# Other SBUF starts for the operands of gate and up: six forms of x and half of the forms of W

## The chip, the cores and the metric

The kernel runs on one core of a Trainium2 chip. The metric is the device time of one execution in microseconds; for the kernel before it is 1454.19 us, the median of three runs between 1452.14 and 1454.41. Engines are named as the profile names them: PE is TensorE, PEld its weight loads, DVE is VectorE, ACT is ScalarE, POOL is GpSimd, SP is SyncE. SBUF is the on-chip memory of 128 partitions; an address in this text is a byte offset within a partition, the same in all of them.

## The reference

A transformer block's two halves over 2048 tokens of 576 channels: linear attention with 32 heads, and a gated feed-forward of width 4608 whose output passes through silu and scales the attention.

```python
xn = _layernorm(x, axis=-1)
s = _A_ref(xn, A_wqkv, A_wo)          # linear attention
g = _silu(_B_ref(xn, B_w_gate, B_w_up, B_w_down))
return x + s * g

def _B_ref(x, w_gate, w_up, w_down):
    g = jnp.einsum("bsd,df->bsf", x, w_gate)
    u = jnp.einsum("bsd,df->bsf", x, w_up)
    h = _gelu(g) * u
    return jnp.einsum("bsf,fd->bsd", h, w_down)
```

All is in float32. The change touches the operands of the two products with `w_gate` and `w_up`.

## The kernel before

Matmuls run in float32r with each operand cut into a high and a low part, so that one product of 288 channels by something is 7 matmuls: a list of seven pairs (`PASSES`: part of W, part of x) over five parts of each operand. The parts of an x form lie behind each other in one tile of 5 x 512 words (2048 bytes a part); a W form has 5 x 128 words (512 bytes a part, 2560 bytes a form).

The stages follow each other on TensorE: k and v for 16 tiles of 128 tokens (`x_mm`, tiles `kv`), q, the attention's output (`s_mm`), then gate and up, then down (`down_mm`, tiles `bd`). All is issued in the program's order: helpers `act`, `vec`, `mm`, `pool` and `dma` (lines 141 to 153) pin each instruction to its place in its engine's stream, and the matmuls of gate and up stand in `product` (line 909).

Gate and up use Strassen's scheme in Winograd's form: for each of 36 matrices (18 groups of 256 columns, for gate and for up) `matrix` runs seven products, each for the two halves s = 1 and s = 0 of the tokens, with 512 columns: 7 x 2 x 7 = 98 matmuls a matrix, 3528 in all. W is the stationary operand, x the moving one. A product takes one of seven forms of W and one of seven forms of x, in this order: A11 with B11 (tile `al`), S2 with T2 (`be`), S1 with T1 (`ga`), S3 with T3 (`de`), A12 with B21 (`al`), S4 with B22 (`ga`), A22 with T4 (`de`). The forms of x are the same for all 36 matrices and stay in SBUF, fourteen tiles: those of s = 1 are named `xo_1_...` and built there (`build`, or `normalize` for the plain ones); those of s = 0 are named `xr_...` and brought back from HBM by `back` (B11, T2, T1, T3 issued by GpSimd, B21, B22, T4 by SyncE). In the profile's names buffer numbers are left out: `xo_T` stands for any T form of s = 1, `xr_T` for any of s = 0.

The forms of W are made anew for each matrix by `mat_sums` (GpSimd) and `cut_w` (ScalarE, VectorE) into two tiles that are used over and over: `wa` holds A11, S1, S2, S3 at places 0 to 3; `wb` holds A12 at place 1, S4 at place 3, and A22 at place 2 or 0 in turn.

SBUF is laid out by hand. `big(i, ...)` places a tile at the numbered place `i` of the pool; what stood there before must be done with first. Places 7 to 10 (`ODD`) start at an odd multiple of 128 bytes, and a tile there that leaves room begins `GAP` = 32 words (128 bytes) later. So all operands of gate, up and down start at a multiple of 256 bytes. `X_SLOT` and `X_BACK` say which form of x stands in which place.

In the k and v stage the moving operand is the weight: tiles `wkv` hold parts of 416 words, 1664 bytes, one behind the other, so that parts 0, 2, 4 start at a multiple of 256 bytes and parts 1, 3, 5 start 128 bytes beyond one. Each of the 16 tiles of tokens has three widths of columns, c = 0, 1, 2 (416, 412 and 388 columns), with 14 matmuls each, seven for each half of the channels. The seven passes read parts 0, 1, 3, 4, 0, 1 and 2 (`KV_PASSES`), so three of seven are off; the sixth piece of weight (c = 2, second half) has no tile of its own and lies in part 5 of the five others, so its seven are all off. Stationary operands (x) all start at multiples of 256 bytes there.

Of the kernel before, what the change touches and what calls it, by code (L numbers as in the profile page):

```python
# [9 lines left out]
F32R = mybir.dt.float32r  # L10
# [6 lines left out]
P = 128  # L17
# [8 lines left out]
TBN = S // TB  # L26
# [9 lines left out]

ODD = (7, 8, 9, 10)
GAP = 32
WP = 320
ODD_W = 9 * HALF  # L40
HEAD_W = 4 * WP + HALF

# [55 lines left out]
def block_kernel(ctx, tc, x, xe, xt, wq_d, wkv_d, wo, wgu_d, wd_d, out):  # L98
    nc = tc.nc
    sb = ctx.enter_context(tc.tile_pool(name="sb", bufs=1))  # L100
# [10 lines left out]
    def fold(t, dims):  # L111
        names = "abc"[: len(dims)]
        return t.rearrange(
            f"p ({' '.join(names)}) -> p {' '.join(names)}", **dict(zip(names[1:], dims[1:]))
        )

    def big(i, shape, dt, name):
        n = 1
        for d in shape[1:]:
            n *= d  # L120
        if i in ODD and n <= ODD_W - GAP:
            t = sb.tile([P, GAP + n], dt, tag=f"b{i}", bufs=1, name=name)
            return fold(t[:, GAP:], shape[1:])
        return sb.tile(shape, dt, tag=f"b{i}", bufs=1, name=name)

    def mid(i, shape, dt, name):
# [22 lines left out]
    def pool(op, *args, **kw):  # L149
        pin(getattr(nc.gpsimd, op)(*args, **kw))  # L150

    def dma(out, in_, eng=None):
        tc.keep_in_program_order((eng or nc.sync).dma_start(out=out, in_=in_))
# [21 lines left out]
    xo, xf, xstat, store = [{}, {}], [{}, {}], {}, {}  # L175

    def load_x(n, k):

        if n % 2 == 0:
            shape = [P, 2, 2, 3 * P] if n < TT else [P, 2, D + 6 * P]  # L180
            xstat[n // 2] = big(14 + n // 2 % 2, shape, F32, f"x_{n}")
        t = xstat[n // 2][:, n % 2 : n % 2 + k]
        if n == 0:
            for j in range(2):
                dma(out=t[:, 0, j], in_=xe[0:P, j], eng=(nc.sync, nc.scalar)[j])
        elif n < TT:
            dma(out=t, in_=xe[n * P : (n + k) * P].rearrange("(t p) j d -> p t j d", p=P))
        else:
            dma(out=t[:, :, 0:D], in_=x[n * P : (n + k) * P].rearrange("(t p) d -> p t d", p=P))
            dma(out=t[:, :, D:], in_=xt[n : n + k].rearrange("t p m -> p t m"))  # L190
# [75 lines left out]
    def new_plain(s, nm):  # L266
        at_ = XM[s][nm]
        xf[s][nm] = (mid if at_ < 3 else big)(at_, [P, 3, TBN], F32, f"xf_{s}_{nm}")

    def normalize(n, s, b, c):  # L270

        if n in xts:
            ms = xts.pop(n)
            m, r = (ms[:, None, i * P : (i + 1) * P] for i in range(2))
        else:
            m, r = rows_of.pop(n)
        xs = xstat[n // 2][:, n % 2, D:].rearrange("p (k t) -> p k t", k=6)
        vec("tensor_sub", xs, xs, m.to_broadcast([P, 6, P]))
        for j, nm in enumerate(BS[b]):
            if nm not in xo[s]:  # L280
                xo[s][nm] = big(2 * b + j, [P, 5, TBN], F32R, f"xo_{s}_{nm}")
                new_plain(s, nm)
            vec(
                "tensor_mul", xf[s][nm][:, :, c], xs[:, 3 * j : 3 * j + 3],
                r.to_broadcast([P, 3, P]),
            )
        for nm in BS[b]:
            to_operand(xo[s][nm], xf[s][nm], c)
# [37 lines left out]
    def to_operand(o, src, c):  # L326
        act(o[:, 0:3, c], src[:, :, c], AF.Copy)
        vec("tensor_sub", o[:, 3:5, c], src[:, 0:2, c], o[:, 0:2, c].bitcast(F32))
        vec("tensor_sub", 
            o[KR : 2 * KR, 2, c], src[KR : 2 * KR, 2, c], o[KR : 2 * KR, 2, c].bitcast(F32)  # L330
        )
# [16 lines left out]
    full = slice(0, TBN)  # L348

    def build(s, nm, i):  # L350
        xo[s][nm] = o = big(i, [P, 5, TBN], F32R, f"xo_{s}_{nm}")
        to_operand(o, xf[s][nm], full)
        return o

# [178 lines left out]
    def run(todo, n=None):  # L533
        for _ in range(len(todo) if n is None else min(n, len(todo))):
            todo.pop(0)()
# [153 lines left out]
    def kv_wo(gi):  # L689

        if gi == 4:
            at["kvh"] = big(4, [P, 4, 2, WP], F32R, "kvh")[:, :, :, 0:HALF]
            at["kvl"] = big(5, [P, 4, 2, WP], F32R, "kvl")[:, :, :, 0:HALF]

            at["kv4"] = big(6, [P, 4, 2, WP], F32R, "kv4")[:, :, :, 0:HALF]
            pool("memset", at["kv4"][Q4:P, 1].bitcast(F32), 0.0)
# [151 lines left out]
    raw, sums, wt = {}, {}, {}  # L848
    X = [{}, xo[1]]
# [235 lines left out]
    def ring(name, make):  # L1085
        if name not in early:
            early[name] = make()
        return early[name]
# [23 lines left out]
    def strided(t):  # L1112
        return bass.AP(
            tensor=t.tensor, offset=t.offset, ap=[list(t.ap[0]), [WP, 5], [1, HALF]]
        )
# [22 lines left out]
    def word_tiles(p):  # L1138
        if p not in word:
            n = len(word)  # L1140
            b = n % 2
            t = ring(("end", b), lambda: big((11, 4)[b], [P, 2, 4, WP], F32R, f"w_end{b}"))
            end = [t[:, i, :, 0:HALF] for i in range(2)]
# [182 lines left out]
    def down_all():  # L1326
# [59 lines left out]
        name=nc.get_next_instruction_name(), engine=mybir.EngineType.Activation,  # L1386
# [23 lines left out]
    _, mv0, st0 = mom[0]  # L1410
# [96 lines left out]
    for n in range(3, 2 * TT):  # L1507
# [3 lines left out]
        if n >= TT:  # L1511
            j, c = divmod(n - TT, 2)
# [18 lines left out]
    def form(nm):  # L1531
        keep(0, nm, build(0, nm, 12))
# [78 lines left out]
    X_BACK = {"B11": 13, "T2": 7, "T1": 8, "T3": 12, "B21": 4, "B22": 5, "T4": 6}  # L1611

    def back(*names, eng=nc.gpsimd):
        for nm in names:
            X[0][nm] = big(X_BACK[nm], [P, 5, TBN], F32R, f"xr_{nm}")
            dma(X[0][nm].bitcast(F32), store[0, nm], eng)

    def first_matrix():
# [5 lines left out]
    q_load(0, 7)  # L1624
    aside = {
        (2, 0): [lambda: den(3), lambda: build(1, "T1", X_SLOT["T1"])],
        (2, 1): [lambda: scale(3, 0, 1), lambda: halve(3, 0, 1)],
        (2, 2): [lambda: scale(3, 2, 3, 4), lambda: halve(3, 2, 3, 4)],
        (2, 3): [lambda: build(1, "T3", X_SLOT["T3"]), lambda: load_mat(0), lambda: q_load(1, 8)],
        (3, 0): [lambda: den(0), lambda: build(1, "T2", X_SLOT["T2"])],  # L1630
        (3, 1): [lambda: scale(0, 0, 1), lambda: halve(0, 0, 1), lambda: back("B11")],
        (3, 2): [lambda: scale(0, 2, 3, 4), lambda: halve(0, 2, 3, 4)],
        (3, 3): [lambda: build(1, "T4", X_SLOT["T4"]), lambda: back("T2")],
        (0, 0): [lambda: den(1)],
        (0, 1): [lambda: scale(1, 0, 1), lambda: halve(1, 0, 1)],
        (0, 2): [lambda: scale(1, 2, 3, 4), lambda: halve(1, 2, 3, 4)],
        (0, 3): [lambda: back("T1"), lambda: mat_sums(0)],
        (1, 0): [lambda: pieces.extend(first_matrix()), lambda: run(pieces[0])],
        (1, 1): [lambda: run(pieces[3])],
    }  # L1640
    pieces = []
    for tb in (2, 3, 0, 1):
        for t in range(TT):
            s_mm(tb, t)
            run(aside.get((tb, t), []))
    wt["b"] = big(14, [P, 4, 5, P], F32R, "wb")
    back("T3")
    run(pieces[4] + pieces[5])
    load_mat(1)
# [70 lines left out]
```

## Time and profile before

| what | value |
|---|---|
| median of the three runs | 1454.19 us |
| the profiled execution's own time | 1452.58 us |
| its span, first to last instruction of the program | 1450.9 us |
| gate and up on TensorE | 276.4 to 1075.8 us |
| down on TensorE | 1076 to 1446 us |
| granted TensorE clock over the span | 1.0 |

A row of the profile's groups names the line, the engine, the operation, what it writes and reads (out<-in), the shape and the count; behind the bar stand the busy time of the group, the mean duration of one in ns, and the idle time of the engine just before. Matmuls overlap on TensorE, so a group's busy time is the union of their durations, and the mean duration of one is longer than the time from one start to the next. A row of the windows view gives a stretch in us, its length, and for each engine (PE, PEld, DVE, ACT, POOL) busy time and count, then the granted clock, the DMA engines' share and GB/s.

### The profile page before, as it was taken

Reading aid. Unit: us, or ns where it says so; the run is one execution under the profiler, and the core shown is the slowest. Engines: PE = TensorE matmul, PEld = TensorE weight load, DVE = VectorE, ACT = ScalarE, POOL = GpSimd, SP = SyncE. Lnnn points to the kernel's source line nnn. Section 1 sums busy time; section 2 is a strip of 40 time slices with the busy share of each in tenths; the row PEclk is TensorE's granted clock in tenths of the full one; section 3 lists DMA queues with packets and bytes.
Section 4 is the critical chain, followed back from the end, with each engine's and each line's share of the span. In section 5 each row is a group of like instructions: output and inputs, shape, how many; then the busy total and the mean of one; then the engine's idle time right before and its main releaser. Section 6 shows DMA issues by size and latency. Waiting matters only on the chain.

```text
span 1450.9 us, 22169 instructions
## 1 busy us (share of the span) xinstructions
PE 1444.4 (100%) x8272; PEld 1286.5 (89%) x8272; DVE 1148.7 (79%) x1609; ACT 565.2 (39%) x918; POOL 580.1 (40%) x520
## 2 busy tenths in 40 slices
PE   9999999999999999999999999999999999999998
PEld 8989989988888888888888888888889999999998
DVE  7688666476787887887777878778888978989898
ACT  6444365333222233322332232332235556555454
POOL 3342340225756567566475754667632000000000
PEclk9999999999999999999999999999999999999999
DMA  5554115521532315224242243323379888767886
GB/s 221 186 205 158 45 36 207 224 95 51 171 101 100 131 52 188 88 95 140 72 159 87 97 150 102 117 87 121 126 272 347 269 261 252 249 188 235 278 293 225
DMA packets 119253, 235.04 MB, mean 162 GB/s; under 512 B 11658, under 2 KB 45354, under 8 KB 117226
## 3 DMA queue, kind: packets, MB, share of 16 engines
q1 hardware_dynamic: 116346, 221.37, 45.4%
q0 software_dynamic: 2656, 12.06, 2.2%
q8 instruction: 65, 1.06, 0.3%
q14 instruction: 42, 0.34, 0.1%
q10 hardware_dynamic: 144, 0.20, 0.0%
HBM read 150.96 MB, written 82.58 MB: 161 GB/s over the span
## 4 chain that ended last, share of the span: by engine, by line
PE 97%; DVE 1%; ACT 1%; issue 0%; POOL 0%; DVEq 0%; ACTq 0%; POOLq 0%
PE bd L147 25%; PE al L909 16%; PE ga L909 16%; PE de L909 16%; PE kv L147 8%; PE be L909 8%; PE s L147 4%; PE q L147 3%; PE kv_a L147 1%; PE idle L147 0%; PE d L147 0%; PE kw L147 0%; PE b L147 0%; ACT e_q L141 0%; PE xt L264 0%
## 5 line engine op out<-in xcount | busy, mean ns | idle before, releaser
L150 POOL TENSOR_TENSOR sm<-raw 128x384 f32<-128x384 f32 x72 | 75.0, 1041 | 144.0 <-DMA raw<-in_wgu_dram 125.8
L147 PE MATMUL kv<-wkv,xo_B 128*128 128x412 f32 (+2 forms) x662 | 125.0, 347 | 0.3 <-ACT xo_B L141 0.3
L147 PEld LDWEIGHTS kv<-wkv,xo_B 128*128 128x128 f32 x662 | 120.2, 188 | 1.7 <-ACT xo_B L141 0.9
L144 DVE TENSOR_TENSOR wa<-sm,wa 128x768 fp32r<-128x768 f32 x72 | 90.5, 1257 | 36.0 <-ACT wa L141 35.2
L147 PE MATMUL bd<-w_head,hi 128*128 128x288 f32 x516 | 117.5, 294 | 0.0
L144 DVE TENSOR_TENSOR wb<-raw,wb 128x256 fp32r<-128x256 f32 (+1 forms) x108 | 103.2, 955 | 7.2 <-ACT wb L141 5.5
L144 DVE TENSOR_TENSOR wa<-raw,wa 128x256 fp32r<-128x256 f32 x72 | 66.8, 928 | 50.6 <-ACT wa L141 47.4
L141 ACT ACTIVATE hi<-raw_h 128x1024 fp32r<-128x1024 f32 x59 | 62.5, 1059 | 96.1 <-PE bd L147 55.7
L147 PE MATMUL bd<-w_end,hi 128*128 128x288 f32 x448 | 89.4, 294 | 0.0
L141 ACT ACTIVATE spot_h<-spot_h 128x512 f32<-128x512 f32 x49 | 30.7, 633 | 150.1 <-DVE spot_h L144 150.1
L147 PEld LDWEIGHTS bd<-w_head,hi 128*128 128x128 f32 x516 | 86.8, 188 | 0.1
L144 DVE TENSOR_TENSOR raw_h<-raw_h,hi 128x1024 fp32r<-128x1024 f32 x59 | 71.8, 1221 | 18.8 <-ACT hi L141 18.8
L141 ACT ACTIVATE wa<-sm 128x1152 fp32r<-128x1152 f32 x36 | 41.8, 1161 | 92.8 <-PE de L909 92.8
L147 PE MATMUL bd<-w_end,raw_h 128*128 128x288 f32 x264 | 77.6, 294 | 0.0
L141 ACT ACTIVATE u<-al 128x512 f32<-128x512 f32 x72 | 41.0, 592 | 90.0 <-PE al L909 60.0
L147 PEld LDWEIGHTS bd<-w_end,hi 128*128 128x128 f32 x448 | 71.6, 188 | 0.0
L147 PE MATMUL bd<-beside,raw_h 128*128 128x288 f32 x240 | 70.5, 294 | 0.0
L150 POOL TENSOR_TENSOR spot_h<-spot_h,spot_h 128x512 f32<-128x512 f32 x45 | 62.8, 1403 | 2.9 <-DVE spot_h L144 2.4
L909 PE MATMUL al<-xo_B,wa 128*128 128x512 f32 x252 | 63.0, 389 | 0.0
L909 PE MATMUL al<-xr_B,wa 128*128 128x512 f32 x252 | 63.0, 389 | 0.0
L909 PE MATMUL be<-xo_T,wa 128*128 128x512 f32 x252 | 63.0, 389 | 0.0
L909 PE MATMUL be<-xr_T,wa 128*128 128x512 f32 x252 | 63.0, 389 | 0.0
(278 smaller groups left out, 4036.8 us busy)
## 6 DMA issues: line engine op xcount, KB each, us to landing
raw_h<-hs SPq DMA_DIRECT2D x176, 256.0 KB
raw<-in_wgu_dram SPq DMA_DIRECT2D x36, 768.0 KB
hs<-spot_h SPq DMA_DIRECT2D x90, 256.0 KB
hs<-spot_g SPq DMA_DIRECT2D x80, 256.0 KB
b<-in_wd_dram SPq DMA_DIRECT2D x42, 432.0 KB
hs<-spot_m SPq DMA_DIRECT2D x38, 256.0 KB
raw_g<-hs SPq DMA_DIRECT2D x22, 256.0 KB
raw_a<-hs SPq DMA_DIRECT2D x20, 256.0 KB
```

Of the source, the lines that this page charges most:

```text
L141: pin(nc.scalar.activation(*args, **kw))
L144: pin(getattr(nc.vector, op)(*args, **kw))
L147: pin(nc.tensor.matmul(*args, **kw))
L150: pin(getattr(nc.gpsimd, op)(*args, **kw))
L909: nc.tensor.matmul(o, w[0:rows, wi, :], xop[0:rows, xi, :], start=(start and n == 0), stop=(n == len(PASSES) - 1), skip_group_check=True,)
```

## The change

`big` takes a gap in words from its caller. A table `X_GAP` gives one for each place in which it matters; the forms of half s = 1 that `build` makes and those that `back` brings use it. Place 7 gets a gap of 0 where it had 32, places 8, 9 and 10 get 8, 16 and 24 words where they had 32, and places 12 and 13 get 8 and 16 where they had none. Tile `wb` is allocated with rows of 672 words for each form instead of 640, and the last 32 words of each are not used.

```diff
+X_GAP = {7: 0, 8: 8, 9: 16, 10: 24, 12: 8, 13: 16}
...
-    def big(i, shape, dt, name):
+    def big(i, shape, dt, name, gap=None):
...
-        if i in ODD and n <= ODD_W - GAP:
-            t = sb.tile([P, GAP + n], dt, tag=f"b{i}", bufs=1, name=name)
-            return fold(t[:, GAP:], shape[1:])
+        if gap is None and i in ODD and n <= ODD_W - GAP:
+            gap = GAP
+        if gap:
+            t = sb.tile([P, gap + n], dt, tag=f"b{i}", bufs=1, name=name)
+            return fold(t[:, gap:], shape[1:])
...
-        xo[s][nm] = o = big(i, [P, 5, TBN], F32R, f"xo_{s}_{nm}")
+        xo[s][nm] = o = big(i, [P, 5, TBN], F32R, f"xo_{s}_{nm}", X_GAP.get(i) if s else None)
...
-            X[0][nm] = big(X_BACK[nm], [P, 5, TBN], F32R, f"xr_{nm}")
+            i = X_BACK[nm]
+            X[0][nm] = big(i, [P, 5, TBN], F32R, f"xr_{nm}", X_GAP.get(i))
...
-    wt["b"] = big(14, [P, 4, 5, P], F32R, "wb")
+    wt["b"] = big(14, [P, 4, 5 * P + 32], F32R, "wb")[:, :, 0 : 5 * P].rearrange(
+        "p f (k c) -> p f k c", c=P
+    )
```

The places themselves stay where they were, and the order of the instructions on every engine, with their waits, stays the same. What moves are the starts, in bytes beyond a multiple of 256:

| operand | place | before | after |
|---|---|---|---|
| T1 of s = 1 (`xo_1_T1`) | 9 | 0 | 192 |
| T3 of s = 1 (`xo_1_T3`) | 10 | 0 | 224 |
| B11 of s = 0 (`xr_B11`) | 13 | 0 | 64 |
| T2 of s = 0 (`xr_T2`) | 7 | 0 | 128 |
| T1 of s = 0 (`xr_T1`) | 8 | 0 | 160 |
| T3 of s = 0 (`xr_T3`) | 12 | 0 | 32 |
| the other eight forms of x | | 0 | 0 |
| W in `wa`, and in `wb` at places 0 and 2 | 15, 14 | 0 | 0 |
| W in `wb` at places 1 and 3 (A12, S4) | 14 | 0 | 128 |

## The prediction

> **What bounds the kernel now.** The page comes first. Its head gives the span; its first part, TensorE's busy time; its clock row, whether the throttle cuts in; its fourth part, the chain of work that ended last.
>
> ```profile
> span 1450.9 us, 22169 instructions
> PE 1444.4 (100%) x8272; PEld 1286.5 (89%) x8272; DVE 1148.7 (79%) x1609; ACT 565.2 (39%) x918; POOL 580.1 (40%) x520
> ...
> PEclk9999999999999999999999999999999999999999
> ...
> PE 97%; DVE 1%; ACT 1%; issue 0%; POOL 0%; DVEq 0%; ACTq 0%; POOLq 0%
> ```
>
> TensorE is busy for 1444.4 of 1450.9 us at full granted clock, and 97% of the chain is matmuls. The view of waits, asked for TensorE alone, shows how little else there is. Its columns are total, times and longest.
>
> ```profile
> PE idle L147 <- POOL ident masks.py:199: 1.6, 1, 1.6
> PE kv L147 <- ACT xo_B L141: 0.3, 1, 0.3
> PE bd L147 <- DVE raw_h L144: 0.2, 1, 0.2
> ```
>
> TensorE waits 2.1 us in all, so the time is the sum of the intervals between matmuls. The windows view over the gate and up stage counts its matmuls and the busy time of each engine there (TensorE, weight loads, VectorE, ScalarE, GpSimd).
>
> ```profile
> 276.40:1075.80 799.40, 799.40 (x3528) 661.91 (x3527) 619.33 (x823) 235.13 (x384) 474.54 (x382) 1.00 0.35 119
> ```
>
> 799.40 us over 3528 matmuls is 226.6 ns each, 55% of the span. One nanosecond on each of them is 3.5 us. VectorE, the busiest helper, has 619.33 us of work there and so 180 us of slack.
>
> **What one matmul costs by its shape.** In the groups kept apart by shape the last figure before the idle time is the mean duration of one matmul. They are pipelined, so a duration is longer than an interval, but what lengthens the stream lengthens both.
>
> ```profile
> L909 PE MATMUL al<-xr_B,wa 128*128 128x512 f32 x252 | 63.0, 389 | 0.0
> ...
> L909 PE MATMUL ga<-xr_T,wa 128*128 128x512 f32 x252 | 63.0, 389 | 0.0
> ...
> L909 PE MATMUL al<-xo_B,wb 128*128 128x512 f32 x252 | 63.0, 389 | 0.0
> ...
> L147 PE MATMUL bd<-w_end,hi 128*128 128x288 f32 x448 | 89.4, 294 | 0.0
> ...
> L147 PE MATMUL kv<-wkv,xo_B 128*128 128x412 f32 x224 | 45.1, 352 | 0.0
> L147 PE MATMUL kv<-wkv,xo_B 128*128 128x416 f32 x214 | 43.2, 352 | 0.3 <-ACT xo_B L141 0.3
> L147 PE MATMUL kv<-wkv,xo_B 128*128 128x388 f32 x224 | 42.1, 338 | 0.0
> ```
>
> All operands of gate, up and down start at a multiple of 256 bytes today, and their durations have no spread: 389 ns whatever form or weight they read. (389 - 294) / (512 - 288) is 0.424 ns a column, which gives an aligned 388-column matmul 336.4 ns, a 412-column one 346.6 and a 416-column one 348.3.
>
> The k and v matmuls are what this trace has of the other kind. Their streamed operand lies in parts 1664 bytes apart, so every second part starts 128 bytes off a multiple of 256. Of the 14 matmuls of a tile with 412 or 416 columns 6 start off; of those with 388 columns 10 do, the last 7 in a row. They measure 338, 352 and 352 ns, which is 1.6, 5.4 and 3.7 ns above the line. The two wider shapes change between on and off inside every run, which gate and up will not do: there a form is streamed 7 times in a row. The nearest rows are therefore the last seven of a 388-column tile, all 128 off. Two such stretches, by tile, with the shortest, median and longest duration:
>
> ```profile
> L147 PE MATMUL kv<-wkv,xo_B x6: 333/336/336, 138.7 to 139.6; 128*128 128x388 f32 x6
> ```
>
> ```profile
> L147 PE MATMUL kv<-wkv,xo_B x4: 341/341/341, 131.5 to 132.1; 128*128 128x388 f32 x4
> ```
>
> The same weight parts in the same order, for two tiles of tokens: one runs at 336 ns, which is the aligned value, the other at 341 ns, 4.6 above it. Within a run the gait hardly changes.
>
> **The change part by part.** No engine's order of instructions changes; only addresses do. Their working, by class:
>
> *x off the grid.* With what each tile's base and gap add up to, T1 of half 1 starts 192 bytes beyond a multiple of 256 and its T3 224; of half 0, B11 starts at 64, T2 at 128, T1 at 160 and T3 at 32. Each is streamed 7 times in each of 36 matrices: 6 x 7 x 36 = 1512 matmuls. The price of one lies between no cost (the run at 336 ns) and 4.6 ns (341 ns), or 0 to 7.0 us in all. Below nothing: the shortest of the rows, 333 ns, is 3.4 under the line; a run that held it would save 1512 x 3.4 = 5.1 us. I take the mean of all 388-column matmuls, 1.6 ns, put on the 10 of 14 that start off: 2.2 ns, so 1512 x 2.2 = **3.3 us**.
>
> *W off the grid.* In the second weight tile the forms now lie 2688 bytes apart, so its places 1 and 3 (A12 and S4) start 128 off. They are stationary operands of 2 x 2 x 7 x 36 = 1008 other matmuls, whose x stays aligned. No matmul of the groups above loads a stationary operand from such a place. If only the distance between the two reads matters, they pay as above, 0 to 4.6 ns; if weight loads hide (661.91 us of them beside 799.40 us of matmuls), nothing; at the 3.4 ns below the line, -3.4 us. I take half of 2.2 ns: **1.1 us**.
>
> *Writers.* ScalarE and VectorE write the moved tiles in the same instructions. The W cuts would have to eat VectorE's 180 us of slack before TensorE waited: nothing. Without that cover a nanosecond there would be one here.
>
> *The four loads of kept forms.* GpSimd issues B11, T2, T1 and T3 of half 0, which get an odd start. By tile, the issue and landing of the three T, and TensorE's first use of two (T1 by ga, T3 by de); then GpSimd's timeline at T1's issue:
>
> ```profile
> L909 PE MATMUL ga<-xr_T,wa x7: 389/389/389, 284.3 to 285.7; 128*128 128x512 f32 x7
> ...
> L909 PE MATMUL de<-xr_T,wa x7: 389/389/389, 287.5 to 288.8; 128*128 128x512 f32 x7
> ...
> L153 POOL DMA_DIRECT2D xr_T<-kept_T x3: 527/536/567, 245.2 to 276.0; - x3
> ...
> DMA to landing us min/median/max: 6.4/6.9/7.8
> ```
>
> ```profile
> 261.97 0.53 POOL L153 DMA_DIRECT2D xr_T<-kept_T  x1 [16.26 <-PE s L147]
> ```
>
> The last, T3, is issued at 276.0 and lands by 283.8 at the latest, 3.7 us before its first matmul at 287.5. T1, issued at 262.0, has 14.5 us to spare, and the two before it are issued earlier still. A landing longer by a third would still be hidden by the matmuls before it: nothing; beyond that each us late is one of TensorE's.
>
> The sum is 3.3 + 1.1 = 4.4 us. The profiled execution took 1452.58 us (its span of 1450.9 and 1.7 around it), so it would become 1457.0; on the median of the runs, 1454.19, which lies 1.6 above it, **1458.6 us**.
>
> **Rivals.** *Addresses don't matter* (not slower). For it: the run at 336 ns pays nothing at 128 off; and the 388-column tiles, which have the largest share of odd starts, are nearest the line, so what the wider ones pay may come from changing parts, or from widths that are no multiple of 64. Against it: the 341 ns stretch, and that only the k and v rows have any spread. Time: 1454.2. The Trainium skill, "SBUF — State Buffer", Specifications (TRN2), has cache lines of 16 bytes as the unit at which a read pays, and under "Who interferes with whom" gives TensorE two read ports that never wait for anyone. All new starts are multiples of 32 bytes, so by that rule every operand crosses as many lines as before and the sum would be 0 instead of 4.4 us. The 336 ns run agrees with it; the 341 ns run doesn't.
>
> *Staggering pays* (faster). The aligned 512-column matmul has 389 - 512 x 0.424 = 172 ns of duration that is not streaming; a part of that may be weight load and stream meeting at the same place, each time alike, as all start on the same grid. If a distance between them took 3.4 ns off, as the 333 ns row shows once, the place would be the 1512 runs with moved x: -5.1 us, **1449.1**; with the 1008 of W, -8.6 us. It decides when weights of the next matmul no longer meet the stream. Against it: it is one of six, and the median of that run is the aligned value.
>
> *A whole further block is read.* If a read went in blocks of 256 bytes (64 columns), an aligned form is 8 blocks and a moved one 9: 64 x 0.424 = 27 ns, times 1512 = 41 us, **1495**. Against it: 388, 412 and 416 columns all touch 7 blocks, on or off the grid, yet 338 is far from 352.
>
> **How the numbers follow.** About 0.2%, 2.9 us, is what a measurement of this kernel can tell from no change. Forecast (moved reads pay 0 to 4.6 ns): 0.55; if all 2520 moved matmuls ran at the slow gait it would be 2520 x 4.6 = 11.6 us, so its own range is 1454.2 to 1465.8, and about 0.10 of it falls within 0.2%. No effect: 0.23. Staggering pays: 0.15, 0.02 of it too small to tell. A further block: 0.07. Slower is thus 0.45 + 0.07 = 0.52, the same 0.10 + 0.23 + 0.02 = 0.35, faster 0.13. The range runs from just above the second rival to the slow gait everywhere with the 2 us by which the runs of before spread: 1449.5 to 1468. It leaves out the further block and the ends of the others.
>
> **What would show it.** Right: in the groups by shape, the ten rows with a moved operand show other means than 389 ns (from wa: al of xr_B, be of xr_T, both ga and both de; from wb: both al and both ga), and the four others don't; the windows view of gate and up grows from 799.40 by some 4 us; the down stage keeps its time. A step is wrong if W's rows stay at 389 (the 1.1 us goes) or if unmoved forms slow down too, since then what counts is the change from run to run. If TensorE's waits grow beyond 2.1 us, a writer or a load is late and the costs that I set at nothing were not. Were all rows at 389, the first rival holds; below it, the second; near 416, the third.

## The result and the profile after

The changed kernel takes 1469.95 us (median of four runs, 1469.58 to 1470.39) where the kernel before takes 1453.74 (four runs, 1452.14 to 1454.41): 1.0113 times as long, with a 95% interval of 1.0096 to 1.0131. The forecast was slower, 1458.6 us, with a range that ended at 1468.0. The direction holds; the size is 16.2 us instead of 4.4.

The windows view of the kernel after, over gate and up and over down (TensorE, weight loads, VectorE, ScalarE, GpSimd, then clock, DMA share and GB/s):

```profile
276.60:1093.20 816.60, 816.60 (x3528) 662.28 (x3527) 622.00 (x824) 235.33 (x384) 473.64 (x382) 1.00 0.34 117
```

```profile
1093.60:1463.90 370.30, 369.72 (x2806) 369.25 (x2805) 330.84 (x384) 194.83 (x237) 19.53 (x26) 1.00 0.83 264
```

Gate and up took 799.40 us before and take 816.60 now, for the same 3528 matmuls at the same clock: 17.2 us, nearly all of the 17.8 by which the profiled span grew (1450.9 to 1468.7 us). Down keeps its time. TensorE's waits in the kernel after:

```profile
PE idle L150 <- POOL ident masks.py:199: 1.6, 1, 1.6
PE bd L150 <- DVE raw_h L147: 0.6, 2, 0.4
PE kv L150 <- ACT xo_B L144: 0.3, 1, 0.3
PE xt L267 <- PE idle L150: 0.3, 1, 0.3
```

They add up to 2.8 us and none lies in gate and up: nothing is late there. The matmuls themselves take longer, as the groups by shape show (busy time in us, then the mean duration of one in ns):

```profile
L912 PE MATMUL al<-xr_B,wb 128*128 128x512 f32 x252 | 64.7, 395 | 0.0
L912 PE MATMUL ga<-xr_T,wa 128*128 128x512 f32 x252 | 64.7, 396 | 0.0
L912 PE MATMUL de<-xo_T,wa 128*128 128x512 f32 x252 | 64.7, 396 | 0.0
...
L912 PE MATMUL be<-xr_T,wa 128*128 128x512 f32 x252 | 64.4, 394 | 0.0
...
L912 PE MATMUL al<-xr_B,wa 128*128 128x512 f32 x252 | 64.2, 394 | 0.0
L912 PE MATMUL be<-xo_T,wa 128*128 128x512 f32 x252 | 63.9, 392 | 0.0
L912 PE MATMUL de<-xo_T,wb 128*128 128x512 f32 x252 | 63.7, 392 | 0.0
L912 PE MATMUL al<-xo_B,wa 128*128 128x512 f32 x252 | 63.0, 389 | 0.0
L912 PE MATMUL de<-xr_T,wb 128*128 128x512 f32 x252 | 63.0, 389 | 0.0
```

All ten rows with a moved operand stand at 394 to 396 ns (five of them shown), whether x moved (by 32, 64, 128, 160, 192 or 224 bytes) or W (by 128). Their busy time is 1.2 to 1.7 us above 63.0, which over 252 matmuls is 4.8 to 6.7 ns each; all ten together lie 15.1 us above, 6.0 ns a matmul. Of the four unmoved rows two stay at 389 and two stand at 392: `be<-xo_T,wa` and `de<-xo_T,wb`, each of which follows a moved run. They add 1.6 us.

These are means. By tile, with the shortest, median and longest duration, one moved run (T2 of s = 0) and one unmoved run (T4 of s = 0):

```profile
L912 PE MATMUL be<-xr_T,wa x7: 387/395/398, 281.4 to 282.8; 128*128 128x512 f32 x7
...
L912 PE MATMUL de<-xr_T,wb x7: 389/389/389, 297.7 to 299.0; 128*128 128x512 f32 x7
```

The seven matmuls of a moved run do not pay alike, and a price per matmul, here and below, is a mean.

### The profile page after: what moved, and what is told of

It reads as the page before. It is cut to its first block, busy times and chain, and to the rows that moved or that the text cites. A ratio compares the mean times of both kernels' runs of the same rounds, so it can differ in the third digit from the quotient of the medians.

```text
span 1468.7 us, 22169 instructions
## 1 busy us (share of the span) xinstructions
PE 1461.6 (100%) x8272; PEld 1286.8 (88%) x8272; DVE 1150.7 (78%) x1609; ACT 565.7 (39%) x918; POOL 578.9 (39%) x520
## 4 chain that ended last, share of the span: by engine, by line
PE 96%; DVE 2%; ACT 1%; issue 0%; DMA 0%; POOL 0%; DVEq 0%; ACTq 0%; POOLq 0%
PE bd L150 23%; PE ga L912 16%; PE al L912 16%; PE de L912 16%; PE kv L150 8%; PE be L912 8%; PE s L150 4%; PE q L150 3%; PE kv_a L150 1%; PE idle L150 0%; PE d L150 0%; PE kw L150 0%; DMA raw_h<-hs 0%; DVE raw_h L147 0%; PE b L150 0%
## 5 line engine op out<-in xcount | busy, mean ns | idle before, releaser
L147 DVE TENSOR_TENSOR wa<-sm,wa 128x768 fp32r<-128x768 f32 x72 | 97.4, 1353 | 36.0 <-ACT wa L144 35.2
L147 DVE TENSOR_TENSOR wb<-raw,wb 128x256 fp32r<-128x256 f32 (+1 forms) x108 | 97.8, 906 | 7.4 <-ACT wb L144 5.8
L912 PE MATMUL al<-xr_B,wb 128*128 128x512 f32 x252 | 64.7, 395 | 0.0
L912 PE MATMUL ga<-xr_T,wa 128*128 128x512 f32 x252 | 64.7, 396 | 0.0
L912 PE MATMUL de<-xo_T,wa 128*128 128x512 f32 x252 | 64.7, 396 | 0.0
L912 PE MATMUL de<-xr_T,wa 128*128 128x512 f32 x252 | 64.6, 395 | 0.0
L912 PE MATMUL ga<-xr_B,wb 128*128 128x512 f32 x252 | 64.5, 395 | 0.0
```

The costliest lines, as they stand in the source:

```text
L147: pin(getattr(nc.vector, op)(*args, **kw))
L912: nc.tensor.matmul(o, w[0:rows, wi, :], xop[0:rows, xi, :], start=(start and n == 0), stop=(n == len(PASSES) - 1), skip_group_check=True,)
```

## The experiments

Three theories were put against each other. **Distance**: what counts is where the weights stand, within 256 bytes, against the stream beside which they are loaded. **Own start**: each operand that is off a multiple of 256 pays for itself. **Change**: what costs is that the place changes from run to run. All times below are medians; the kernel before ran on the same chip each time.

### x alone and W alone

The kernel after with one of its two parts undone:

```diff
 # x alone: the kernel after with
-    wt["b"] = big(14, [P, 4, 5 * P + 32], F32R, "wb")[:, :, 0 : 5 * P].rearrange(
-        "p f (k c) -> p f k c", c=P
-    )
+    wt["b"] = big(14, [P, 4, 5, P], F32R, "wb")
 # W alone: the kernel before with the reverse of this
```

> The six forms of x as in the change, the forms of W back at 2560 bytes. The changed kernel spends 17.2 us more on 2520 moved matmuls, 6.8 ns each. Theory 'distance' (a matmul pays when its moving operand and the stationary operand that is loaded beside it start at different places within 256 bytes): 1512 x 6.8 = 10.3 us more than before, 1464; the rows of the six moved runs at 394 to 396 ns, those from wb at 389 but for the one behind a moved run. Theory 'own start' (each operand off a multiple of 256 pays for itself): the same. Theory 'change' (what costs is that the place within 256 bytes changes from run to run): also some 10 us, but then runs of unmoved forms behind moved ones pay as much as moved ones.

> The forms of W 2688 bytes apart, all forms of x on multiples of 256. 'Distance' and 'own start': 1008 x 6.8 = 6.9 us more than before, 1460.6; the four rows of A12 and S4 at 394 to 395 ns, the others at 389 but for runs behind moved ones. My prediction had 1.1 us for this part. A sum of this and of the kernel with x alone near 17 us says that the two parts add up.

x alone takes 1464.49 us against 1453.26 (1.0076, 1.0059 to 1.0093), W alone 1459.02 (1.0040, 1.0025 to 1.0055): 11.2 and 5.8 us. They add up to 17.0, beside 16.2 for the whole change. With x alone the six moved rows stand at 394 to 396 ns and are 9.1 us of busy time above 63.0, 6.0 ns on each of 1512 matmuls; another 2.2 us lie in two unmoved rows right behind moved ones, `be<-xo_T,wa` (393 ns) and `al<-xo_B,wb` (394 ns). With W alone the four rows of A12 and S4 stand at 394 to 396 ns and all others at 389 to 391; 5.8 us is 5.7 ns on each of 1008.

W alone also shows which weights a stream meets. The places to look at are those where a run with weights on the grid (at multiples of 256 bytes) gives way to one with weights off, and back. First the timeline of W alone where S3 with `xr_T` (on) gives way to A12 (off), with start and duration in us; then the groups by shape in two windows of 0.07 us, at that place and where S4 (off) gives way to A22 (on):

```profile
512.71 0.62 PE L909 MATMUL de<-xr_T,wa 128*128 128x512 f32 x2
512.94 0.19 PEld L909 LDWEIGHTS al<-xo_B,wb 128*128 128x128 f32 x1
```

```profile
L909 PE MATMUL al<-xo_B,wb 128*128 128x512 f32 x1 | 0.4, 405 | 0.0
L909 PE MATMUL de<-xr_T,wa 128*128 128x512 f32 x1 | 0.4, 397 | 0.0
```

```profile
L909 PE MATMUL ga<-xr_B,wb 128*128 128x512 f32 x1 | 0.4, 390 | 0.0
L909 PE MATMUL de<-xo_T,wb 128*128 128x512 f32 x1 | 0.4, 389 | 0.0
```

The load for A12's first matmul begins at 512.94, while the last matmul of S3 streams. That matmul's own weights and x are on the grid, and it takes 397 ns. The last matmul of S4 works with weights that are off, while those loaded beside it are on the grid: 390 ns. Over the 36 matrices the last matmul of S3 takes 397 ns on average and the last of S4 takes 390. So a matmul pays for the weights of the **next** one.

### Everything shifted, and all of W shifted

```diff
 # everything 128 bytes later: the kernel before with
-    eps_t = sb.tile([P, 32], F32, name="eps_t")
+    eps_t = sb.tile([P, 64], F32, name="eps_t")
```

```diff
 # all forms of W 128 bytes later: the kernel before with
-        wt["a"] = big(15, [P, 4, 5, P], F32R, "wa")
+        t = big(15, [P, 32 + 4 * 640], F32R, "wa")[:, 32:]
+        wt["a"] = t.rearrange("p (f n) -> p f n", f=4)[:, :, 0 : 5 * P].rearrange(
+            "p f (k c) -> p f k c", c=P
+        )
 # and the same for wb
```

> The kernel before with its first small tile 128 bytes larger: every SBUF tile behind it moves by 128 bytes, so all operands of gate, up, down, q and s start 128 bytes beyond a multiple of 256, moving and stationary alike, and the distance between them stays. 'Distance': as before, 1453.7 within 2 us, gate and up at 389 ns. 'Own start': 3528 x 6.8 = 24 us more in gate and up alone, 1478 or later. 'Change': as before.

> The kernel before with both W tiles begun 128 bytes later: every stationary operand of gate and up starts 128 beyond a multiple of 256, every moving one on it, and nothing changes from run to run. 'Distance' and 'own start': 3528 x 6.8 = 24 us more, 1478; all fourteen rows at 394 to 396 ns. 'Change': as before, 1453.7, at 389 ns.

With everything shifted the time is 1453.41 against 1453.26 us: 1.0001 (0.9991 to 1.0010). With W alone shifted it is 1472.76: 1.0138 (1.0123 to 1.0153). The windows views of gate and up, first everything shifted, then W:

```profile
276.00:1076.00 800.00, 799.77 (x3529) 662.20 (x3528) 629.21 (x823) 235.54 (x384) 473.96 (x382) 1.00 0.35 119
```

```profile
276.00:1095.40 819.40, 819.40 (x3528) 665.20 (x3527) 622.66 (x824) 235.03 (x384) 472.60 (x382) 1.00 0.34 116
```

All operands 128 bytes off a multiple of 256 cost nothing as long as they are off together. 'Own start' would have put 24 us or more there and falls. With W alone shifted every run stands at the same distance, and the stage is 20.0 us longer, 5.7 ns a matmul. All fourteen rows read as this one:

```profile
L909 PE MATMUL be<-xr_T,wa 128*128 128x512 f32 x252 | 64.4, 395 | 0.0
```

Single matmuls lie between 389 and 405 ns there, so 395 is again a mean. 'Change' would have put nothing there and falls too. Distance is left.

### The price at 288 columns

```diff
 # the words of down 288 apart: the kernel before with
 WP = 320
+WD = 288
...
-            tensor=t.tensor, offset=t.offset, ap=[list(t.ap[0]), [WP, 5], [1, HALF]]
+            tensor=t.tensor, offset=t.offset, ap=[list(t.ap[0]), [WD, 5], [1, HALF]]
...
-            t = ring(("end", b), lambda: big((11, 4)[b], [P, 2, 4, WP], F32R, f"w_end{b}"))
+            t = ring(("end", b), lambda: big((11, 4)[b], [P, 2, 4, WD], F32R, f"w_end{b}"))
```

> The words of the down stage lie 288 words apart, not 320, so the moving operand of 1248 of its 2808 matmuls starts 128 bytes off the grid while the stationary one stays on it; gate and up as before. 'Distance', with the 5.5 ns that each matmul of gate and up paid with all W 128 off: 1248 x 5.5 = 6.9 us more than before, 1460.2; rows of down with odd words above 294 ns. With the 1.6 to 2.2 ns that the prediction took from the 388-column rows: 2.0 to 2.7 us more. If shorter streams pay nothing: 1453.3.

1455.23 against 1453.07 us, 1.0012 (1.0002 to 1.0022). Windows over down, this kernel first, then the kernel before:

```profile
1076.20:1448.10 371.90, 371.79 (x2806) 371.44 (x2806) 331.32 (x384) 194.66 (x237) 19.98 (x26) 1.00 0.83 264
```

```profile
1076.20:1446.30 370.10, 369.92 (x2808) 369.46 (x2807) 331.56 (x384) 194.63 (x237) 20.07 (x26) 1.00 0.82 264
```

1.9 us over the 1248 matmuls that moved is 1.5 ns each, a quarter of what the same 128 bytes cost at 512 columns. That lies just below the 1.6 to 2.2 that the prediction took from the 388-column rows. It is a small difference: the interval of the ratio leaves 0.3 to 3.2 us.

### Other distances

Two scans and three more kernels move W alone, by giving its tiles other gaps and other pitches (`g` words ahead, `p` words from form to form, in the edit above):

```diff
 # first scan:   wa g=0 p=656, wb g=0  p=644
 # second scan:  wa g=0 p=652, wb g=0  p=641
 # third scan:   wa g=0 p=660, wb g=44 p=648
 # all of W by 16, 144 or 192 bytes:  g = 4, 36 or 48, p=640
```

> Only the forms of W move, x stays on multiples of 256: S1 starts 64 bytes off, S2 128, S3 192, A12 16, S4 48, A22 32 or 0 in turn, A11 0. 'Any distance pays': all rows but those of A11 at 394 to 396 ns (A22, half on the grid, some 392), the total near that of the kernel with all W 128 off, less a seventh for A11 and a fourteenth for A22: 19.5 x 11/14 = 15.3 us more than before. 'The price grows with the distance up to 128': A12 (16) and S4 (48) nearer to 389, S2 (128) highest.

> Only the forms of W move: S1 starts 48 bytes off, S2 96, S3 144, A12 4, S4 12, A22 8 or 0 in turn, A11 0. 'Any distance pays': 15.3 us more than before, all moved rows at 394 to 396 ns. 'Only the distance within 256 counts and small ones are near to none': the rows of A12, S4 and A22 at 389 to 390, and 19.5 x 6/14 = 8.4 us more. If distances below 16 bytes cost more than those of 16 and up, these three rows stand above 396.

> The kernel before with every form of W begun 144 bytes off a multiple of 256, x on it. In the second scan S3 stood at 144 and its 504 matmuls took 389 ns, as on the grid, though every other distance paid. 'The distance alone sets the price': 1453.3, all fourteen rows at 389 ns. 'History' (a run can keep the gait that it came in with, and S3 came in with a good one): some of the 20 us of the kernel with all W 128 off, rows between 390 and 396.

> Every form of W 16 bytes off, x on the grid. The first scan had A12 at 16 with 395 to 396 ns. 'The distance alone sets the price': 6.5 ns on 3528 matmuls, 23 us more, 1476, all rows at 395 to 396 ns. 'Only the distance within 128 bytes counts' (144 is 16 beyond 128): as the kernel with all W 144 off.

> Every form of W 192 bytes off, x on the grid. The first scan had S3 at 192 with 392 to 393 ns. 'The distance alone sets the price': 3.3 ns on 3528 matmuls, 11.6 us more, 1465. 'History': a row value other than 392 to 393, anywhere from 389 to 396.

> Only the forms of W move, to the distances not yet seen: S1 80 bytes off, S2 160, S3 240, A12 208, S4 16 (272), A22 176 or 240 in turn, A11 0. If a distance exists at which the next weights hide better than on the grid, its row stands below 389 ns and shows a faster version. 'Zero is the floor': no row below 389; most at 392 to 397, some 15 us more than before.

The scans took 1469.95 (1.0113, 1.0093 to 1.0133), 1467.75 (1.0098, 1.0078 to 1.0118) and 1467.08 us (1.0091, 1.0071 to 1.0111). W by 16 bytes takes 1476.79 (1.0158, 1.0137 to 1.0178), by 144 bytes 1476.41 (1.0158, 1.0141 to 1.0175), by 192 bytes 1460.85 (1.0047, 1.0031 to 1.0063).

From the groups by shape, first of the second scan: S2 at 96 bytes, S4 at 12, A12 at 4, S1 at 48, A22 at 0 or 8, S3 at 144.

```profile
L909 PE MATMUL be<-xr_T,wa 128*128 128x512 f32 x252 | 65.0, 397 | 0.0
...
L909 PE MATMUL ga<-xo_B,wb 128*128 128x512 f32 x252 | 64.6, 394 | 0.0
...
L909 PE MATMUL al<-xo_B,wb 128*128 128x512 f32 x252 | 64.5, 394 | 0.0
L909 PE MATMUL ga<-xr_T,wa 128*128 128x512 f32 x252 | 64.4, 395 | 0.0
...
L909 PE MATMUL de<-xo_T,wb 128*128 128x512 f32 x252 | 63.6, 391 | 0.0
...
L909 PE MATMUL de<-xo_T,wa 128*128 128x512 f32 x252 | 63.0, 389 | 0.0
```

Then the same run of S3 where all of W is 144 off, and where all of it is 192 off:

```profile
L909 PE MATMUL de<-xo_T,wa 128*128 128x512 f32 x252 | 64.6, 396 | 0.0
```

```profile
L909 PE MATMUL de<-xo_T,wa 128*128 128x512 f32 x252 | 63.5, 392 | 0.0
```

And the lowest and the highest row of the third scan (S3 at 240 bytes, S4 at 16):

```profile
L909 PE MATMUL ga<-xo_B,wb 128*128 128x512 f32 x252 | 64.7, 396 | 0.0
...
L909 PE MATMUL de<-xr_T,wa 128*128 128x512 f32 x252 | 63.0, 389 | 0.0
```

Three things follow. Even 4 bytes of distance cost nearly as much as 128: A12 stands at 394 ns right behind the free run of S3. So there is no small distance that is nearly none, and the theory that the price grows with the distance up to 128 missed. The price has no simple law that these distances show: 16 and 144 cost most where all of W stands there (22.8 us and more), 192 a third of that. And the distance alone doesn't fix it: at 144 bytes S3 ran for free in the second scan, and at 396 ns where all of W was there. The sharp form of the theory, one price for each distance, falls with that.

In those two kernels S3 lies at the very same bytes of `wa` (3 x 652 words are as many as 36 + 3 x 640), and x stands at the same places too; what differs is where the other forms of W lie. So the same run can keep more than one gait, that is, pace. What ran ahead is the likeliest cause, though no run changes it alone. It isn't simply the gait of the run ahead, as the expectation for 144 bytes has it: S1, right before S3 in the second scan, stood at 395 ns. In the third scan S3 at 240 bytes is at 389 to 390 ns as well, also behind a slow S1 (395), and no kernel with all of W at 240 was run. What picks the gait stays open. No row of any kernel here is below 389 ns, so none of the distances tried makes a version faster than the kernel before.

## Why the prediction was wrong

**The bound held.** TensorE's matmuls make the time, in gate and up as in down; its waits are 2.8 us against 2.1.

**The mechanism held, its price did not.** Moved operands pay, in every moved run, and the count of 2520 was right. The step that failed is the price of one: "1.6 ns, put on the 10 of 14 that start off: 2.2 ns", from the 388-column rows. It is the term that was mis-sized, in both places: for x 3.3 us were forecast and x alone measured 11.2; for W 1.1 us, from half that price, and W alone measured 5.8. With 5.7 ns, which all of W 128 off shows, the 2520 matmuls would have come to 14.4 us. The rows of the kernel after give 6.0 ns, 15.1 us, and 1.6 us more in the two unmoved runs behind moved ones, which the sum had at nothing.

Two choices made it small. First, the 388-column rows were carried over to 512 columns as they were. At 288 columns the price is 1.5 ns and at 512 it is 5.7, both at 128 bytes, so a price from a narrower stream is no upper end for a wider one; the slow gait of 4.6 ns, which I took as the end of the range, was below what all moved rows then showed. Whether it is the width alone, or also that the words of down change between on and off as they are read, isn't settled: one width in one stage was tried. The trace of the kernel before had a sign that more was possible: the 412-column matmuls stand 5.4 ns above the line with 6 of 14 off, which is 12.6 ns for each of those, and were set aside because the place changes inside their runs. Second, the weights were counted at half because they might hide beside the stream. They are the other half of the matter: what counts is where the next weights stand against the stream beside which they are loaded. How the two reads hinder each other inside SBUF or TensorE no run here shows.

**What I set at nothing was nothing.** VectorE is busy for 622.00 us in the stage after and 619.33 before, and TensorE waits for none of it. The loads of kept forms, by tile in the kernel after (issue and landing of the T forms, first use of T3):

```profile
L912 PE MATMUL de<-xr_T,wa x7: 393/394/397, 287.9 to 289.3; 128*128 128x512 f32 x7
...
L156 POOL DMA_DIRECT2D xr_T<-kept_T x3: 530/536/570, 245.4 to 276.2; - x3
...
DMA to landing us min/median/max: 6.4/7.2/8.7
```

T3 is issued at 276.2, lands by 284.9 at the latest and is used at 287.9.

**The rivals.** 'Addresses don't matter' is wrong; what misled is that the 336 ns stretch was one of two gaits. The Trainium skill, "TensorE: Matmul & The Clock Gate", under "Step-by-step: what each phase is for", says that loading the next weights takes no read bandwidth from the running matmul, as TensorE has a read port for each. This case doesn't agree: the matmul beside the first load of A12 took 397 ns instead of 389, and W alone shifted made the stage 20.0 us longer. The 16-byte lines that the Trainium skill has in "SBUF — State Buffer", Specifications (TRN2), don't give it either: with all of W 16 bytes off, a whole line, the kernel was 23.2 us longer, the most of any distance tried. 'Staggering pays' is wrong at all distances tried: no row lies below the grid's 389 ns. 'A whole further block' would have shown rows near 416 ns; they stand at 394 to 396.

That two unmoved rows slowed down I had named as a sign that the change from run to run counts. It does, but only as an aftermath: with all of W 128 off nothing changes from run to run, and every run pays.

## What to carry to other kernels

Where matmuls follow each other with a new stationary operand each, lay out both operands so that the next weights and the stream that they are loaded beside start at the same place within 256 bytes. Two such places were tried, all on multiples of 256 and all 128 bytes beyond, with float32r operands, and they cost the same. What such a thing costs should be measured at the stream's own width: 1.5 ns at 288 columns and 5.7 at 512 here. A uniform price in rows that move together, with no wait, points to the reads themselves.

## What the runs showed of the hardware that I had not expected

- The rate of a float32r matmul depends on addresses modulo 256 bytes, by the distance between the stream and the next weights: 226.6 ns from start to start on average at distance 0, and with all of W off 5.7 ns more at 128, some 6.5 more at 16 and 144, 2 more at 192. Both operands 128 off together cost nothing.
- It is the weights of the next matmul that count: with them off, a matmul on the grid took 397 ns; with its own off and the next on, 390.
- Matmuls in a row have gaits: S3 at the same bytes, 144 off, ran at 389 or 396 ns, depending on where the other forms of W lay, and in k and v of the kernel before the same weights, streamed 128 off beside two tiles of tokens, ran at 336 or 341 ns.
